# Stage B on eight narrow array tiles, with the complex products added on GpSimd

## The chip, the core and the metric

The kernel runs on one core of one Trainium2 chip. A core has a matrix engine (TensorE; PE in the profile, and PEld for its weight loads), three engines for elementwise work (VectorE: DVE, ScalarE: ACT, GpSimd: POOL), and SyncE (SP), which here only starts transfers. Transfers can be started from SP, ACT or POOL; 16 DMA engines carry all of them. Each engine takes its instructions in the order in which the program gives them, and waits where an operand is not ready. Matmul results land in PSUM, eight banks of 128 x 512 fp32. GpSimd cannot read PSUM, so what it is to work on has to be copied to SBUF first.

The metric is the device time of one execution in microseconds, as the median of some runs.

## The reference

```python
def _attn_ref(x, filt_r, filt_i):              # x: (8, 3008, 256)
    X = np.fft.rfft(x, axis=1)
    Y = X * (filt_r + 1j * filt_i)[None, :, :]  # filters: (1505, 256)
    return np.fft.irfft(Y, n=x.shape[1], axis=1)

def _moe_ref(x, w_gate, w_val, w_out):          # x: (24064, 256), d_ff = 1536
    gate = np.maximum(x @ w_gate, 0.0)
    return (gate * (x @ w_val)) @ w_out
```

Each of the eight batches is filtered along its 3008 positions through a real Fourier transform. Its 3008 x 256 result then goes, as rows, through a gated two-layer network. The output has 24064 rows of 256 fp32 values.

## The kernel before, in words

**Stages.** 3008 is split as 94 x 32. Stage A transforms along the 94, as matmuls by a cosine and sine table; its result goes through a DRAM buffer (`Abuf`) and comes back transposed as the tile `at`. Stage B, for each of 48 values of the first frequency, transforms along the 32, multiplies with the filter (a complex product) and transforms back; the result goes through a second DRAM buffer (`Dbuf`). Stage C transforms back along the 94 and writes `yT`, which is the input of the network (FFN). The FFN works in 47 blocks of 512 positions.

**Order.** The order of all work is written out by hand. After an opening (batch 0 through stages A, B and C, and the loads of weights, up to line 647), the main loop (line 689) has 47 blocks of 12 steps. One step issues `gv` (line 504: two matmuls into `psV`, two into `psG`, a copy of psV to `vsb` on ACT, and max and product into `prod` on DVE), then `o_part` (line 522: four matmuls into `psO` for the block before), and then whatever the dictionary `side` holds for that step. At steps 8 and 10 of a block, after that, `item_c` (stage C, into `psY`, line 487) makes the next block's input. `at_step(s, f)` puts work f at step s. Each batch b from 1 on has a step `end`, 72 steps after that of the batch before it, and its stages are placed by their distance to it (lines 663 to 687):

- Loads: `next_x` (line 669) at four steps, 79 to 115 steps ahead of `end`. It waits on POOL for the latest prod (`hold_gpsimd`, line 271), issues a chunk's six transfers from POOL (`load_chunk`, line 321), and then folds the chunk before it (`fold_chunk`, line 334).
- Folding: six POOL operations on a chunk of 128 x 2048 fp32, two of 128 x 1024 elements (lines 339, 340) and four of 128 x 512 (lines 341 to 344), one directly after the other.
- Stage A: `tiled_a` (line 347) four times a batch, 32 matmuls each on 32x32 tiles of the array, four copies (ACT and DVE), four stores to Abuf from SP.
- Stage B: `fwd` (line 390) at six steps, six apart (five for batch 1): eight matmuls on 64x64 tiles of the array into two banks `psX`. `product` (line 401) at that step and the next three: each is one DVE multiplication of a bank with a filter table, into `tt` (by `Ftr`) or `uu` (by `Fti`). `inv` (line 418) at the step of the next fwd: 16 matmuls, eight by `I2t` on tt and eight by `I2u` on uu, accumulated in two banks `psD`, two copies on ACT to `dsb`; every second one ends in a store to Dbuf from SP.
- `load_d` (line 466) two steps ahead of `end`: eight transfers from Dbuf on SP.

The real and imaginary rows of a filter lie twice in Ftr and Fti, as the layout of psX asks for it; in the opening `place_filter` (line 249) makes the second copy, by SP transfers, one ACT and one POOL copy. The inverse tables I2t and I2u are made in the opening from the forward table `F2` by matmuls (`make_back_t`, `make_back_u`).

**PSUM.** `bank` (line 153) gives out the eight banks in turn, the one longest free first; `done` returns a bank at its last reader in program order. psO holds one for six steps, gv takes two in each step.

**Batch 0** goes through stage B in the opening in `first_b` (line 447). It uses the same matmuls, but eight of its products are made on POOL, from copies `xs` that ACT makes of psX. Between its rounds `amid` issues some stage-A work of batch 1 (`items_a`, line 296), which reads the tiles `XF` that SP loads (`load_x`).

Of the kernel before, what the change touches and what calls it, by code (L numbers as in the profile page):

```python
# [29 lines left out]
N1, N2 = 94, 32  # L30
# [11 lines left out]
def _tables():  # L42
# [5 lines left out]
    m1 = np.zeros((NROW, N1))  # L48
# [3 lines left out]
    own = np.zeros((128, 2, 2, 64))  # L52
    order = np.arange(64).reshape(2, 32).T.reshape(64)
    for hg in range(48):
        g, a = divmod(hg, 2)
        rows = slice(a * 64, a * 64 + 64)
        e, j = g % 2, 12 * a + g // 2
        rt, ra, rm = 64 * e + j, 128 + 4 * j + 2 * e, 48 * e + j
        f = np.zeros((64, 64))
        t = np.zeros((64, 64))  # L60
        u = np.zeros((64, 64))
        k1 = 1 + g + 24 * a if hg != 47 else 0
        th = 2 * np.pi * (((n1 - 23) * k1) % N1) / N1
        wa[part, rt] = wa[part, ra] = np.cos(th)
        if k1 not in (0, 47):
# [4 lines left out]
            conj = np.tile([1.0, -1.0], 16)  # L70
            th = 2 * np.pi * (np.outer(n2, k) % S) / S
            c, s = np.cos(th), np.sin(th)
            f[:] = np.block([[c, -s], [s, c]])
            ct, st = c.T, s.T
            t[:] = np.block([[ct, st], [-st, ct]])
            u[:] = np.block([[-st, ct], [-ct, -st]]) * np.concatenate([conj, conj])[:, None]
        else:
            m1[rm] = np.cos(th) / S
            th = 2 * np.pi * (np.outer(n2, k1 + N1 * p) % S) / S
            c, s = np.cos(th), np.sin(th)  # L80
            f[0:32, 0:32:2] = c
            f[0:32, 32::2] = -s
            t[0:32:2, 0:32] = 2.0 * c.T
            t[32::2, 0:32] = -2.0 * s.T
            u[0:32:2, 0:32] = -2.0 * s.T
            u[32::2, 0:32] = -2.0 * c.T
            if k1 == 0:
                sign = np.where(n2 % 2 == 0, 1.0, -1.0)
                f[0:32, 32] = sign
                t[0, 0:32] = 1.0  # L90
                t[32, 0:32] = sign
                u[0] = 0.0
                u[32] = 0.0
        f2[lo + 64 * e, j] = f
        if g >= NG - 2:
            own[rows, 0, g - NG + 2], own[rows, 1, g - NG + 2] = t[:, order], u[:, order]
# [4 lines left out]
    swap = np.zeros((128, 128))  # L101
    conj = np.where(r % 2 == 0, 1.0, -1.0)
    swap[r ^ 32, r] = conj * np.where(r & 32, -1.0, 1.0)
    m1 = np.concatenate([m1, np.zeros((128 - NROW, N1))])
    fold = np.zeros((128, 4, 32))
    i = np.arange(24)
    for odd in range(2):
        k1 = 2 - odd + 2 * (i % 12) + 24 * (i // 12)
        if not odd:
            k1[k1 == 48] = 0  # L110
# [5 lines left out]
    tab = np.concatenate([perm, swap, own.reshape(128, -1), m1], 1)  # L116
# [4 lines left out]
def kernel(  # L121
# [52 lines left out]
    M1 = consts.tile([NROW, N1], BF16)  # L174
    F2 = consts.tile([128, NG, 64], BF16)
    I2t = consts.tile([128, NG, 64], BF16)
    I2u = consts.tile([128, NG, 64], BF16)
    Ftr = consts.tile([128, NG, D], BF16)
    Fti = consts.tile([128, NG, D], BF16)
# [15 lines left out]
    H = NG // 2  # L195
    FILT = ((filt_r, Ftr), (filt_i, Fti))
    tabs = pro.tile([128, tab_h.shape[1]], BF16, tag="tabs", bufs=1)
    perm, swap = tabs[:, 0:64], tabs[:, 64:192]

    def make_back_t(q):  # L200

        psI = [bank("psI", 4, 64) for _ in range(2)]
        for e in range(2):
            for a in range(2):
                for j in range(4):
                    nc.tensor.matmul(psI[e][64 * a:64 * a + 64, j],
                                     F2[64 * e:64 * e + 64, 12 * a + 4 * q + j, :],
                                     perm[64 * e:64 * e + 64], start=True, stop=True,
                                     tile_position=(64 * e, 64 * a))
        for e in range(2):  # L210
            nc.vector.tensor_copy(I2t[:, 8 * q + e:8 * q + 8:2, :], psI[e])
            done(psI[e])

    def make_back_u(q):

        psI = bank("psI", 8, 64)
# [39 lines left out]
    def place_nyq():  # L256
        for (src, dst), n in zip(FILT, nyq):
            nc.gpsimd.tensor_copy(dst[96:97, NG - 1, :], n)
# [471 lines left out]
```

## Time and profile before

| what | value |
|---|---|
| median of 3 runs (lowest, highest) | 891.53 us (890.38, 891.91) |
| span of the profiled execution | 885.7 us |
| around the span, to the median | 5.8 us |
| mean granted TensorE clock | 0.997 |
| first psV of the FFN at | 52.3 us |
| last output matmuls (L530) end near | 880 us |
| one batch of 72 steps in the steady part | 107 us |
| HBM | 60.42 MB read, 48.23 MB written |

The profile is of one execution on the chip, and times in it are counted from its first instruction. It gives no total for that execution beside its span, so its own time is taken as the span and the 5.8 us that lie between it and the median of the runs. In a line of it, "L433 PE MATMUL psD<-tt,I2t 64*64 64x256 bf16 x4" means: four matmuls issued by line 433, into psD, from tt and I2t, with 64 rows and 64 columns of the array, 256 columns long. What stands in brackets behind a line is how long its engine stood idle ahead of it, and whom it waited for. The start of a matmul is recorded and its end is modelled, so the cost of a group is read from its start to the start of the next one.

### The profile page before, as it was taken

Reading aid. Unit: us, or ns where it says so; the run is one execution under the profiler, and the core shown is the slowest. Engines: PE = TensorE matmul, PEld = TensorE weight load, DVE = VectorE, ACT = ScalarE, POOL = GpSimd, SP = SyncE. Lnnn points to the kernel's source line nnn. Section 1 sums busy time; section 2 is a strip of 40 time slices with the busy share of each in tenths; the row PEclk is TensorE's granted clock in tenths of the full one; section 3 lists DMA queues with packets and bytes.
Section 4 is the critical chain, followed back from the end, with each engine's and each line's share of the span. In section 5 each row is a group of like instructions: output and inputs, shape, how many; then the busy total and the mean of one; then the engine's idle time right before and its main releaser. Section 6 shows DMA issues by size and latency. Waiting matters only on the chain.

```text
span 885.7 us, 19147 instructions
## 1 busy us (share of the span) xinstructions
PE 872.1 (98%) x7190; PEld 506.9 (57%) x7190; DVE 575.7 (65%) x875; ACT 495.2 (56%) x882; POOL 376.4 (43%) x375
## 2 busy tenths in 40 slices
PE   8989999999999999999999999999999999999997
PEld 3435655666555665556655665556655666666665
DVE  4866766676666676667765776657766577655553
ACT  5734555556555655556555556555655555555552
POOL 4654796147631667216780186803866000000001
PEclk9999999999999999999999999999999999999999
DMA  9994466533645337533376234663446512421111
GB/s 242 304 221 98 155 142 146 141 117 96 150 133 124 98 101 184 129 98 98 103 179 145 81 111 133 165 125 86 123 132 142 118 46 63 105 56 31 38 34 50
DMA packets 106067, 107.28 MB, mean 121 GB/s; under 512 B 20167, under 2 KB 90087, under 8 KB 105334
## 3 DMA queue, kind: packets, MB, share of 16 engines
q1 hardware_dynamic: 81286, 76.03, 33.5%
q0 software_dynamic: 23792, 29.16, 13.3%
q8 instruction: 57, 0.93, 0.4%
q10 hardware_dynamic: 896, 0.86, 0.3%
q14 instruction: 36, 0.29, 0.1%
HBM read 60.42 MB, written 48.23 MB: 123 GB/s over the span
## 4 chain that ended last, share of the span: by engine, by line
PE 92%; DMA 4%; DVE 1%; ACT 1%; issue 0%; POOL 0%; SPq 0%; ACTq 0%; DVEq 0%
PE psV L509 27%; PE psO L530 27%; PE psG L509 26%; PE psF L353 3%; PE psY L493 2%; PE psD L433 2%; PE psX L396 2%; DMA dC<-Dbuf 2%; DMA WoT<-in_moe_w_out_dram 1%; PE psA L282 1%; DVE AT L291 1%; PE psA L303 1%; PE psJ L565 0%; DMA Dbuf<-dsb 0%; DMA Dbuf<-AS 0%
## 5 line engine op out<-in xcount | busy, mean ns | idle before, releaser
L514 DVE SCALAR_TENSOR_TENSOR prod<-psG,vsb 128x512 bf16<-128x512 f32 x564 | 388.8, 690 | 262.4 <-ACT vsb L512 257.1
L512 ACT CAST vsb<-psV 128x512 bf16<-128x512 f32 x564 | 331.9, 589 | 266.5 <-PE psV L509 179.4
L509 PE MATMUL psV<-yT,WvT 128*128 128x512 bf16 x1128 | 337.6, 380 | 0.6 <-DVE yT L500 0.6
L530 PE MATMUL psO<-WoT,prod 128*128 128x256 bf16 x2256 | 336.7, 273 | 1.1 <-DMA WoT<-in_moe_w_out_dram 1.1
L509 PE MATMUL psG<-yT,WgT 128*128 128x512 bf16 x1128 | 335.8, 379 | 0.2 <-ACT yT L498 0.2
L530 PEld LDWEIGHTS <-prod 128*128 128x128 bf16 x2256 | 220.6, 98 | 144.8 <-issue 1.5
L509 PEld LDWEIGHTS <-WgT 128*128 128x128 bf16 x1128 | 110.1, 98 | 135.6 <-issue 2.5
L509 PEld LDWEIGHTS <-WvT 128*128 128x128 bf16 x1128 | 98.6, 98 | 41.3 <-issue 30.3
L274 POOL CAST scr<-prod 128x8 f32<-128x8 bf16 x24 | 4.5, 189 | 245.0 <-DVE prod L514 245.0
L554 POOL DMA_DIRECT2D out_dram<-osb x5 | 2.6, 536 | 195.7 <-ACT osb L543 195.7
L543 ACT COPY osb<-psO 128x512 f32<-128x512 f32 x92 | 53.9, 586 | 25.9 <-PE psO L530 23.5
L412 DVE TENSOR_TENSOR tt<-psX,Ftr 128x512 bf16<-128x512 f32 x96 | 65.0, 680 | 1.6 <-POOL uu L410 0.6
L339 POOL TENSOR_TENSOR fold<-XP 128x1024 f32<-128x1024 f32 x24 | 56.5, 2354 | 19.9 <-PE psF L353 18.8
L412 DVE TENSOR_TENSOR uu<-psX,Fti 128x512 bf16<-128x512 f32 x88 | 59.8, 680 | 0.0
L326 POOL DMA_DIRECT2D XP<-in_x_dram x96 | 57.6, 603 | 3.0 <-PE psG L509 1.6
L340 POOL TENSOR_TENSOR XP<-XP 128x1024 f32<-128x1024 f32 x24 | 56.3, 2348 | 2.0
L441 ACT CAST dsb<-psD 128x512 bf16<-128x512 f32 x94 | 50.6, 591 | 11.0 <-PE psD L433 11.0
L498 ACT CAST yT<-psY 128x512 bf16<-128x512 f32 x47 | 27.5, 586 | 31.0 <-PE psY L493 30.8
L360 DVE CAST asb<-psF 128x512 bf16<-128x512 f32 x48 | 30.9, 686 | 18.6 <-PE psF L353 18.6
L360 ACT CAST asb<-psF 128x512 bf16<-128x512 f32 x48 | 25.8, 589 | 30.5 <-PE psF L353 30.5
L493 PE MATMUL psY<-M,dC 96*128 96x94 bf16 (+18 forms) x604 | 37.7, 198 | 2.8 <-DMA dC<-Dbuf 2.8
L493 PEld LDWEIGHTS <-dC 96*128 96x128 bf16 x604 | 34.4, 97 | 7.2 <-DMA dC<-Dbuf 3.2
(80 smaller groups left out, 500.9 us busy)
## 6 DMA issues: line engine op xcount, KB each, us to landing
XP<-in_x_dram POOLq DMA_DIRECT2D x48, 256.0 KB, 5.8
Dbuf<-dsb SPq DMA_DIRECT2D x23, 512.0 KB
dC<-Dbuf SPq DMA_DIRECT2D x57, 192.0 KB
XP<-in_x_dram POOLq DMA_DIRECT2D x96, 96.0 KB, 2.6
Abuf<-asb SPq DMA_DIRECT2D x96, 96.0 KB
at<-Abuf SPq DMA_DIRECT2D x24, 384.0 KB
out_dram<-osb SPq DMA_DIRECT2D x69, 94.0 KB
XF<-in_x_dram SPq DMA_DIRECT2D x15, 256.0 KB
```

The source lines that it names most:

```text
L326: nc.gpsimd.dma_start(xp[r:r + 24, 0:4:2, :], _ap(x, (b * N1 * N2 + o) * D, [[N2 * D, 24], [47 * N2 * D, 2], [1, 512]]))
L339: tt(t, xp[:, 0:2], xp[:, 2:4], op=ALU.add)
L340: tt(xp[:, 2:4], xp[:, 0:2], xp[:, 2:4], op=ALU.subtract)
L360: copy(asf[:, :, q, :], banks[q])
L412: nc.vector.tensor_tensor(p, psX, filt, op=ALU.mult)
L441: copy(dsb[:, a, o:o + 2, :], psD[a])
L493: nc.tensor.matmul(psY[:, o:o + w], dCs[b, n2 // 8][:, n2 % 8, h * 128:(h + 1) * 128], M1[:, n1:n1 + w], start=True, stop=True)
L509: nc.tensor.matmul(pt[:, :W], w[:, h, ft * 128:(ft + 1) * 128], yt[:, h, :], start=(h == 0), stop=(h == 1))
L512: nc.scalar.copy(vsb, psV[:, :W])
L514: nc.vector.scalar_tensor_tensor(prod, in0=psG[:, :W], scalar=0.0, in1=vsb, op0=ALU.max, op1=ALU.mult)
L530: nc.tensor.matmul(psO[:, t % 2], prods[ft][:, t * 128:(t + 1) * 128], WoT[:, ft, :], start=(ft == 0), stop=(ft == NFT - 1))
L543: copy(osb[:, t0 % 2:t % 2 + 1], psO[:, t0 % 2:t % 2 + 1])
```

## The change

- **Forward (batches 1 to 7).** Three forwards a batch instead of six. Each is 32 matmuls on eight 64x32 tiles, real and imaginary part in separate banks: four banks, for two halves e of the rows and two parts. ACT copies the two banks of e=1 to SBUF (`xs`, fp32) and gives them back at once.
- **Products and adds.** Eight DVE products a forward, one in each of eight successive steps, now with fp32 result (`qr`). After each second one POOL adds or subtracts the pair into `y` (bf16). So y is the finished complex product.
- **Inverse.** Three a batch, ten steps after their forward: 32 matmuls on eight 32x64 tiles, one pass over y with one table IT, into four banks; two ACT and two DVE copies, one store.
- **Batch 0** keeps products without adds, on the new tiles: four terms a pair with tables IT and its negative ITN.
- **Filters** are stored once, with 20 POOL transfers in two halves; no copies, no extra rows. The tables are made by `make_back`, on PE, DVE and ACT. Two small SP transfers (`hold_sync`) hold the loads of batch 1's x behind the filters.
- **Folding.** A chunk is loaded by four transfers of 128 rows, at steps of its own; its six POOL operations are spread over eight steps (at 0, 2, 4, 5, 6, 7), in a new order, in place. The clearing of XP (four memsets) goes.

```diff
-    def place_filter(fi, a, half, copy):
...
+    def make_back():
+        psI = {}
+        for t in range(2):
+            for e in range(2):
+                psI[t, e] = bank("psI", 3, 2, 64)
...
+            for e in range(2):
+                gs = slice(6 * t + e, 6 * t + 6, 2)
+                nc.vector.tensor_copy(IT[:, gs], psI[t, e])
+                nc.scalar.mul(ITN[:, gs], psI[t, e][:, :, 0], -1.0)
...
+    def hold_sync(tile_):
+        scr = sb.tile([128, 32], BF16, tag="scs", bufs=2)
+        nc.sync.dma_start(scr[:tile_.shape[0]], tile_)
...
     def load_chunk(b, j):
-        xp = XP[j]
-        for q in range(4):
...
+        xp, o = XP[j], (b * N1 * N2 + 2 * j) * D
+        for i in range(4):
+            up = N2 * D if i % 2 == 0 else -N2 * D
+            nc.gpsimd.dma_start(xp[:, i, :],
+                                _ap(x, o + (46 * (i % 2) + 47 * (i // 2)) * N2 * D,
+                                    [[8 * D, 4], [up, 32], [1, 512]]))
+    def fold_steps(b, j):
+        xp, st = XP[j], {}
+        tt = nc.gpsimd.tensor_tensor
+        def differences():
+            st["d"] = fs.tile([128, 2, 512], FP32, tag="fold", bufs=1, name="fold")
+            tt(st["d"], xp[:, 0:2], xp[:, 2:4], op=ALU.subtract)
+        yield differences
+        yield lambda: tt(xp[:, 0:2], xp[:, 0:2], xp[:, 2:4], op=ALU.add)
+        yield lambda: tt(xp[:, 2], xp[:, 0], xp[:, 1], op=ALU.add)
+        yield lambda: tt(xp[:, 3], xp[:, 0], xp[:, 1], op=ALU.subtract)
+        yield lambda: tt(xp[:, 0], st["d"][:, 0], st["d"][:, 1], op=ALU.add)
+        yield lambda: tt(xp[:, 1], st["d"][:, 0], st["d"][:, 1], op=ALU.subtract)
...
+    def fwd(b, r):
+        ps_ = psXs[b, r] = {(e, comp): bank("psX", 2, D) for e in range(2) for comp in range(2)}
+        for m in range(2):
+            for comp in range(2):
+                for cg in range(4):
+                    for e in range(2):
+                        forward(b, ps_[e, comp][32 * cg:32 * cg + 32, m], 6 * cg + 2 * r + m, comp, e, cg)
+        for comp in range(2):
+            xs = fs.tile([128, 2, D], FP32, tag="xs", bufs=2, name="xs")
+            nc.scalar.copy(xs, ps_[1, comp])
+            done(ps_[1, comp])
+            ps_[1, comp] = xs
+    def product(b, r, e, n):
+        comp, k = ((0, 0), (1, 1), (0, 1), (1, 0))[n]
+        p = fs.tile([128, 2, D], FP32, tag="qr", bufs=6, name="qr")
+        nc.vector.tensor_tensor(p, psXs[b, r][e, comp], FILT[k][1][:, 4 * r + e:4 * r + e + 3:2, :], op=ALU.mult)
+        qr[n % 2] = p
+        if n % 2:
+            y = fs.tile([128, 2, D], BF16, tag="y", bufs=6, name="y")
+            nc.gpsimd.tensor_tensor(y, qr[0], qr[1], op=ALU.add if n // 2 else ALU.subtract)
...
+    def inv(b, r):
+        psD = [bank("psD", 2, D) for cg in range(4)]
+        dsb = sb.tile([128, 4, 2, D], BF16, tag="dsb", bufs=3, name="dsb")
+        for m in range(2):
+            inverse(b, psD, r, m, ((0, 0), (1, 1)))
+        evacuate(dsb, psD, slice(0, 2))
...
+        store_d(b, r, dsb, 0, 2)
...
+    hold_sync(Fi[:, 5, D - 32:])
+    load_x(1, nc.sync, ((0, 0, 4 * q),))
+    hold_sync(Fi[:, 11, D - 32:])
     load_x(1, nc.sync, ((1, 0, 4 * q),))
...
         if b > 1:
-            for j, e in enumerate((-74, -69, -62, -55) if b == 2 else (-74, -69, -64, -57)):
-                l = (22, 29, 34, 43)[j] if b == 2 else end - 115 + NFT * j
...
+                at_step((12, 20, 29, 40)[j] if b == 2 else end + (-134, -120, -104, -90)[j], next_x)
+                l = (20, 31, 42, 53)[j] if b == 2 else end + (-124, -109, -94, -81)[j]
+                for n, f in zip((0, 2, 4, 5, 6, 7), fold_steps(b, j)):
+                    at_step(l + n, f)
+                e = (-74, -68, -62, -55)[j] if b == 2 else (-74, -69, -64, -57)[j]
                 at_step(end + e, lambda b=b, j=j: tiled_a(b, j))
             at_step(end + e + 4, lambda b=b: load_at_tiled(b))
...
+        for r in range(3):
+            lf, li = ((-36, -26), (-25, -15), (-14, -4))[r] if b == 1 else ((-38, -28), (-26, -16), (-14, -4))[r]
+            at_step(end + lf, lambda b=b, r=r: fwd(b, r))
+            for n in range(8):
+                at_step(end + lf + n, lambda b=b, r=r, n=n: product(b, r, n // 4, n % 4))
+            at_step(end + li, lambda b=b, r=r: inv(b, r))
```

`forward` issues one matmul on a 64x32 tile; `inverse` issues, for each table and part, eight matmuls on the eight 32x64 tiles (four groups of rows, two of columns), the parts in the order real, imaginary; `evacuate` copies four banks, ACT and DVE in turn. Where two pieces of work have the same step, that of the lower batch comes first.

## The prediction

> **What bounds the kernel now.** I read the page's busy shares first, then the chain that ended last, then the busy time by stretch, and last the instructions in order of time on PE and on POOL.
>
> From the page: busy time by engine, and the chain by engine.
>
> ```profile
> PE 872.1 (98%) x7190; PEld 506.9 (57%) x7190; DVE 575.7 (65%) x875; ACT 495.2 (56%) x882; POOL 376.4 (43%) x375
> ...
> PE 92%; DMA 4%; DVE 1%; ACT 1%; issue 0%; POOL 0%; SPq 0%; ACTq 0%; DVEq 0%
> ```
>
> One batch takes 107 us in the steady part. Busy time by stretch there (stretch, length, then PE, PEld, DVE, ACT, POOL, the granted clock, DMA):
>
> ```profile
> 334.00:441.00 107.00, 107.00 (x929) 62.74 (x928) 71.94 (x111) 61.64 (x111) 53.62 (x51) 1.00 0.48 122
> ```
>
> PE has no idle time in it. So an edit gains only PE time, and it loses as soon as PE has to wait for anything. PE in order of time (start, then duration of the merged group):
>
> ```profile
> 405.24 0.60 PE L530 MATMUL psO<-WoT,prod 128*128 128x256 bf16 x4
> 405.77 0.41 PE L396 MATMUL psX<-at,F 64*64 64x256 bf16 x8
> 406.01 0.28 PE L433 MATMUL psD<-tt,I2t 64*64 64x256 bf16 x4
> ...
> 406.34 0.28 PE L433 MATMUL psD<-uu,I2u 64*64 64x256 bf16 x4
> 406.55 0.60 PE L509 MATMUL psV<-yT,WvT 128*128 128x512 bf16 x2
> ...
> 407.43 0.60 PE L530 MATMUL psO<-WoT,prod 128*128 128x256 bf16 x4
> 407.86 0.59 PE L509 MATMUL psV<-yT,WvT 128*128 128x512 bf16 x2
> ...
> 441.50 0.30 PE L433 MATMUL psD<-tt,I2t 64*64 64x256 bf16 x4
> ...
> 442.06 0.61 PE L509 MATMUL psV<-yT,WvT 128*128 128x512 bf16 x2
> ```
>
> Start to start: an output group followed by psV takes 0.43-0.44 us, followed by a tiled group 0.53, so entering costs 0.09. An FFN step is 1.30 (406.55 to 407.86). Eight psX matmuls take 0.24 ahead of psD; alone, the trace has 0.35. Sixteen psD matmuls take 0.54 behind psX and 0.56 (441.50 to 442.06) alone. Four matmuls on four 64x64 tiles cost 0.11 together.
>
> POOL in order of time, one chunk's loads and its folding:
>
> ```profile
> 437.92 0.19 POOL L274 CAST scr<-prod 128x8 f32<-128x8 bf16 x1 [3.62 <-DVE prod L514]
> 439.72 2.41 POOL L326 DMA_DIRECT2D XP<-in_x_dram  x4 [1.62 <-PE psG L509]
> 442.13 1.40 POOL L330 DMA_DIRECT2D XP<-in_x_dram  x2
> 446.08 2.35 POOL L339 TENSOR_TENSOR fold<-XP 128x1024 f32<-128x1024 f32 x1 [2.55 <-PE psF L353]
> 448.51 2.35 POOL L340 TENSOR_TENSOR XP<-XP 128x1024 f32<-128x1024 f32 x1
> 450.94 1.27 POOL L341 TENSOR_TENSOR XP<-fold 128x512 f32<-128x512 f32 x1
> 452.28 1.29 POOL L342 TENSOR_TENSOR fold<-fold 128x512 f32<-128x512 f32 x1
> ```
>
> A wide fold operation occupies POOL 2.43 us start to start, a narrow one 1.34, a 256 KB load 0.70 of issue. Today only tiled_a, many steps later, waits for POOL.
>
> **PE work of stage B.** Per batch now: 7 entries into tiled mode (0.65), psX 5 x 0.242 + 0.345 = 1.56, psD 5 x 0.539 + 0.563 = 3.26; together 5.47 us. After: three forward groups of 32 matmuls on eight 64x32 tiles and three inverse groups of 32 on eight 32x64 tiles, never adjacent. If eight run in the 0.11 that four take, each is four such rounds, the lone psD group's 0.563, plus 0.093 to enter: 6 x 0.656 = 3.94. Gain 1.53, over seven batches **-10.7 us**. The bound on the other side is four at a time: each group then has four more rounds, 1.09, the six 6.56, a loss of 1.1 a batch, +7.6. I take the gain, since psF, on sixteen 32x32 tiles, needs 1.07 us for 32 fp32 matmuls of 512 columns (chain) where psA needs 3.43 for 8: those tiles do run together.
>
> The Trainium skill, "TensorE: Matmul & The Clock Gate" (its section "Wait — 56ns, not 53.3ns?"), speaks against this: start to start never drops below about 25 ns, so 32 small matmuls would need 0.80 us. The trace disagrees, with psD starts 3 ns apart within a round. By the rule six groups would cost an estimated 6 x (0.09 + 0.80 + 0.10) = 5.9 and the gain would turn into a loss of about 3 us in all.
>
> **The new link: PE waits for POOL.** The inverse now reads y, which POOL adds from two DVE products. Four adds per group, each priced by the 1.34 of L341 (L410, one bf16 input, is 1.16; the choice moves 0.2 an add). They enter the queue that already carries folds and loads, and the inverse that waits holds up every matmul behind it, hence ACT's vsb, DVE's prod and all output.
>
> Work one steady group, r=0 of batch b-1, while batch b (3 to 7) is folded. A chunk's loads are now four issues instead of six (2.8 us for 3.8), moved to other steps than its folding. Count steps from its forward (end-110 in b's counting), time 0 at that step's first matmul. Step 1 starts at 1.96; two stage-C items add 0.25 each; the inverse at step 10 wants all four adds at about 15.7. DVE's second, fourth, sixth and eighth product are ready at 5.1, 7.1, 9.7, 12.3 (prod about 1.25 us into a step, ACT first copying two xs at 0.48 a piece, DVE at 0.61 an operation; the DVE lines come at that spacing in first_b). POOL's order by the due steps, with the end of each: y0 6.4 | differences 8.8, y1 10.2 | sums 12.6, y2 13.9 | narrow 15.3 | narrow 16.6, hold and four loads 19.7 (0.25 + 4 x 0.70) | y3 21.05. **PE stands 5.3 us.** Without those loads it would be 2.3; without the folds it would be zero (y3 at 15.4). For r=1 the same tally ends at 0.2, for r=2 at none: fewer folds lie before y3. Five batches (b-1 = 2 to 6): 5 x 5.5 = 27.5. Batch 1, with its own due steps and one load set in each group: 2.2, 2.4, 2.4, together 7.0. Batch 7 has no folding beside it: 0. Sum **+34.5**.
>
> **What such a wait does to the clock.** Near 50 us PE waits 2.35 us for dC; the stretches around it:
>
> ```profile
> 48.20:50.40 2.20, 0.00 (x0) 0.00 (x0) 0.67 (x1) 0.00 (x0) 0.00 (x0) 1.00 1.02 312
> 51.41:54.82 3.41, 3.41 (x8) 1.06 (x7) 1.47 (x3) 0.68 (x2) 3.41 (x6) 0.50 0.88 125
> ```
>
> The clock is then 0.50 for 3.41 us, a loss of up to 1.7. Each of the eight long waits costs between 0 and 1.7 (13.6 in all); how much of the half-clock stretch falls into the wait itself is open, so I take the middle, **+6.8**.
>
> **DVE, ACT and PSUM.** DVE keeps 24 products a batch, now eight steps in a row: 2 x 0.61 per 1.30 step fits. Six of twelve dsb copies move there (6 x 0.61). ACT loses six and gains six xs copies. A forward takes four banks at once, but two return after the xs copies. SP still stores three slabs of Dbuf a batch. Cost zero, covered by DVE's 65%; if the cover fails, a lag of about 0.3 us for 21 forwards, +6.
>
> **End of batch 1.** Its last inverse comes one step later (end-4 for end-5), and psY already waits 0.45 us for dC there: **+1.3** (0 if earlier loads free the DMAs). Other batches keep end-4.
>
> **The opening, before the first psV at 52.** Filters take 20 POOL issues instead of 12 (8 x 0.55 = 4.4 us); the last ends near 23, before psX at 28. Six SP copies, two 2.7 us filter copies, the memsets and make_back_u (0.65) go; that gains nothing while the transposes (4.2 each) follow the last psA, paced by XF. The 7.1 us XP memset lies beside FFN steps. Two small SP transfers now hold the second batch's XF loads behind half the filters, and XF[0] goes as one piece; the first item reads it at 29.2, so 0 to 2 late. Forward and inverse change tile shape in each round, about 0.1-0.2 x 5. Bounds -1 and +4; I take **+1**.
>
> **Sum.** -10.7 + 34.5 + 6.8 + 1.3 + 1.0 = +32.9. The profiled span is 885.7; launch and end add 5.8 to the median 891.5 of the three runs. 891.5 + 32.9 = 924.
>
> **Rivals.**
> - *POOL keeps up* (other sign). y3 lands before the inverse because POOL's issue and adds overlap more than their rows. For it: POOL is busy only 43%. Against it: the rows follow each other without overlap, and 16 us of POOL work stands where 10.6 fit. It decides once that work shrinks by a third. Then -10.7 + 2.3 = 883; partial waits reach up to 905.
> - *DVE blocks POOL's port.* Half of the products now read two SBUF operands, which no row here does beside POOL. If POOL stood still for their four 0.61 us, 2.4 us more in some thirteen groups that are already late or nearly so: +31, 955; half of it is 940. The Trainium skill's "GPSIMD Engine Reference" (section 1, Specifications) names such contention with two SBUF inputs. In the trace a fold stays at 2.35 beside PSUM-reading DVE work, which tests it not.
> - *Tiles run four at a time.* +7.6 for -10.7 turns 924 into 942; the psF row speaks against it.
>
> **Chances.** Forecast 0.50 (own range 908 to 936), POOL keeps up fully or in part 0.33, port 0.11, four at a time 0.06. The keeping-up case splits into 0.29 under 889.7, little within 0.2% of the median (about what a measurement of this kernel can tell from no change), the rest above. The range 882 to 940 leaves out about a tenth at each end. Faster 0.28, same 0.03, slower 0.69.
>
> **What would show it.** Right: PE waiting on POOL's y in the list of waits, some 5 us at one inverse per batch and nothing in the last batch; POOL's load issues between the third and fourth add; the clock at 0.50 after them; groups of 32 at 0.56. Wrong: no such wait, POOL's y starting straight after its product, or tiled groups of 0.8 us and more. The weakest step is the price of POOL's queue.

## The result, and the profile after

The changed kernel takes 959.85 us (median of 4 runs, 957.96 to 964.30) where the kernel before takes 891.53: 1.077 times as long, interval 1.073 to 1.081. The forecast was 924, with 940 as the upper end of its range. The direction was right, the size was not: 68 us came where 33 were expected. The profiled execution has a span of 956.2 us against 885.7, so 70.5 us are to be found in the trace. A run that lies over 1.5% above the fastest of its kernel counts as slow and is left out of a median; this concerns four runs of one experiment below.

The page of the changed kernel: busy time by engine, the granted clock in 40 slices, and the chain by engine.

```profile
PE 883.8 (92%) x7593; PEld 507.7 (53%) x7715; DVE 665.9 (70%) x917; ACT 488.9 (51%) x879; POOL 463.0 (48%) x412
...
PEclk9899999998999989999999989999899999999999
...
PE 57%; POOL 14%; issue 12%; DVE 8%; DMA 6%; ACT 2%; SPq 0%; ACTq 0%; POOLq 0%; DVEq 0%
```

PE carried 92% of the chain before and carries 57% now; POOL, DVE and "issue" have come in. DVE is busy for 90 us more (575.7 before). Its 50 copies of psD (the evacuation that moved there) take 31 us of that; the rest must be operations that have become longer. The clock is below its highest digit in five slices.

The waits of PE in the changed kernel (who waited for whom: us in total, times, longest):

```profile
PE psD L351 <- POOL y L451: 25.9, 7, 4.8
PE psD L351 <- DVE prod L519: 10.8, 20, 1.2
PE psV L514 <- DVE yT L505: 6.6, 3, 4.0
PE psX L340 <- DMA at<-Abuf: 4.4, 1, 4.4
```

The first line is the one that the prediction asked for. The next two name DVE, which the prediction had put at nothing, and the fourth is a transfer that it did not mention.

**One steady inverse, r = 0 of batch 5.** POOL in order of time:

```profile
554.13 1.27 POOL L451 TENSOR_TENSOR y<-qr 128x512 bf16<-128x512 f32 x1 [9.63 <-DVE qr L447]
555.36 2.36 POOL L292 TENSOR_TENSOR fold<-XP 128x1024 f32<-128x1024 f32 x1
557.66 1.73 POOL L451 TENSOR_TENSOR y<-qr 128x512 bf16<-128x512 f32 x1
559.35 2.80 POOL L294 TENSOR_TENSOR XP<-XP 128x1024 f32<-128x1024 f32 x1
562.11 1.71 POOL L451 TENSOR_TENSOR y<-qr 128x512 bf16<-128x512 f32 x1
563.79 1.71 POOL L295 TENSOR_TENSOR XP<-XP 128x512 f32<-128x512 f32 x1
565.46 1.26 POOL L296 TENSOR_TENSOR XP<-XP 128x512 f32<-128x512 f32 x1
566.67 0.18 POOL L231 CAST scr<-prod 128x8 f32<-128x8 bf16 x1
566.80 2.70 POOL L281 DMA_DIRECT2D XP<-in_x_dram  x4
569.52 1.27 POOL L451 TENSOR_TENSOR y<-qr 128x512 bf16<-128x512 f32 x1
```

This is the order of the prediction's tally to the letter: the fourth sum stands behind two narrow folds, the hold and four loads. But four of the ten have grown, a sum from 1.27 to 1.73 or 1.71, a wide fold from 2.36 to 2.80, a narrow one to 1.71.

PE in order of time, at that inverse and at the next one (r = 1):

```profile
565.62 0.37 PE L351 MATMUL psD<-y,IT 32*64 32x256 bf16 x9 [0.30 <-DVE prod L519]
570.84 0.85 PE L351 MATMUL psD<-y,IT 32*64 32x256 bf16 x20 [4.84 <-POOL y L451]
...
575.54 0.63 PE L340 MATMUL psX<-at,F 64*32 64x256 bf16 x32
576.10 0.61 PE L514 MATMUL psV<-yT,WvT 128*128 128x512 bf16 x2
...
590.09 0.29 PE L351 MATMUL psD<-y,IT 32*64 32x256 bf16 x1
591.45 0.29 PE L351 MATMUL psD<-y,IT 32*64 32x256 bf16 x2 [1.07 <-DVE prod L519]
592.04 0.73 PE L351 MATMUL psD<-y,IT 32*64 32x256 bf16 x29 [0.30 <-DVE prod L519]
```

A gap is read here from start to start of neighbouring matmuls inside the group. At r = 0 it is 5.11 us in each of batches 2 to 6. The psX group of 32 takes 0.56 from its start to psV, as forecast. At r = 1 PE does not wait for a sum at all: of the four banks that psD was given, one was psG two steps ago and one was psG a step ago, and `prod`, the DVE operation that reads them, is late. So two gaps follow each other, 1.36 and 0.59 us, in each of the five batches. At r = 2 the longest gap is 0.59 in four batches and 1.42 in one.

Why DVE is late stands in its own order of time, at the products of that r = 1 and with POOL's beside them:

```profile
581.35 0.68 DVE L519 SCALAR_TENSOR_TENSOR prod<-psG,vsb 128x512 bf16<-128x512 f32 x1
581.95 1.38 DVE L447 TENSOR_TENSOR qr<-xs,Fr 128x512 f32<-128x512 f32 x1
583.25 0.68 DVE L519 SCALAR_TENSOR_TENSOR prod<-psG,vsb 128x512 bf16<-128x512 f32 x1
583.85 2.23 DVE L447 TENSOR_TENSOR qr<-xs,Fi 128x512 f32<-128x512 f32 x1
...
588.57 2.23 DVE L447 TENSOR_TENSOR qr<-xs,Fr 128x512 f32<-128x512 f32 x1
590.72 1.27 DVE L519 SCALAR_TENSOR_TENSOR prod<-psG,vsb 128x512 bf16<-128x512 f32 x2
```

```profile
582.74 2.80 POOL L292 TENSOR_TENSOR fold<-XP 128x1024 f32<-128x1024 f32 x1
586.23 1.26 POOL L451 TENSOR_TENSOR y<-qr 128x512 bf16<-128x512 f32 x1 [0.69 <-DVE qr L447]
587.45 2.79 POOL L294 TENSOR_TENSOR XP<-XP 128x1024 f32<-128x1024 f32 x1
```

A product of two SBUF operands begins at 583.85 and ends at 586.08, half a microsecond after the fold that began at 582.74 has ended (585.54). The fold began while the product before it (581.95 to 583.33) still ran, and took 2.80. So each seems to hold until the other is through. The whole trace bears this out: 68 of the 84 products from xs begin while a fold or sum runs on POOL, and 65 of them end 0.55 us after that operation's end; of the other 16, 14 take 0.67 to 0.68. Folds and sums that begin while such a product runs mostly take 0.3 to 0.5 us more (37 of 40), the others keep to 1.25 to 1.28 or 2.34 to 2.36. Over the whole trace, by groups (line, engine, operation, operands, count, then busy time and mean ns):

```profile
L447 DVE TENSOR_TENSOR qr<-xs,Fr 128x512 f32<-128x512 f32 x42 | 66.6, 1585 | 0.0
...
L447 DVE TENSOR_TENSOR qr<-xs,Fi 128x512 f32<-128x512 f32 x42 | 59.1, 1406 | 0.0
...
L447 DVE TENSOR_TENSOR qr<-psX,Fr 128x512 f32<-128x512 f32 x42 | 28.8, 685 | 8.1 <-PE psX L340 7.0
```

The same multiplication takes 0.685 us from PSUM and 1.4 to 1.6 from SBUF in the mean. The 84 products from SBUF hold some 68 us more of DVE than at 0.68 a piece. In batch 7, where there is nothing to fold, products from xs are 0.68 long when POOL stands still and 1.45 when a sum runs.

**The clock behind the long gap.** Busy time by stretch (stretch, length, PE, PEld, DVE, ACT, POOL, the granted clock, DMA share, GB/s):

```profile
564.74:570.84 6.10, 0.96 (x13) 0.34 (x13) 2.03 (x4) 0.58 (x1) 6.08 (x9) 0.71 0.33 72
570.84:574.14 3.30, 3.08 (x27) 1.56 (x28) 1.81 (x3) 1.61 (x3) 2.38 (x2) 0.50 1.01 183
574.14:577.84 3.70, 3.65 (x51) 2.03 (x50) 1.64 (x4) 2.15 (x4) 0.00 (x0) 1.00 1.00 191
```

Between 1.3 and 4.1 us after PE falls idle in each gap of 5.11 us, the clock goes to 0.50 for 6.83 us. Here about half of that lies in the gap and 3.3 us behind it; in the other batches 3.7 to 6.0 us lie behind it. The sum over the trace of (1 - clock) times PE's busy time, taken in short pieces, comes to 14.2 us after the first psV; before, the same sum gives 1.3.

**The account.** First psV: 61.5 for 52.3, +9.2. First psV to the last output group: 890.3 for 827.4, +62.9. Behind it: -1.6. The list of waits understates the inverses: it counts a wait from the modelled end of the matmul before it, about 0.3 us after that matmul's start. Read from start to start instead, from each inverse's first matmul to the next piece of work, the 21 inverse groups hold 50.0 us above 0.57 a piece, where the list has 36.7. With that, the 62.9 are the gain in PE work (-10.7), the inverses (+50.0), the waits for yT and for `at` (+11.0) and the clock while PE works (+12.9 by the sum above). These make 63.2; the half clock inside an inverse is counted twice in it.

### The profile page after: what moved, and what is told of

Same layout as the page of the kernel before. It is cut to its first block, busy times and chain, and to the rows that moved or that the text cites. A ratio compares the mean times of both kernels' runs of the same rounds, so it can differ in the third digit from the quotient of the medians.

```text
span 956.2 us, 20067 instructions
## 1 busy us (share of the span) xinstructions
PE 883.8 (92%) x7593; PEld 507.7 (53%) x7715; DVE 665.9 (70%) x917; ACT 488.9 (51%) x879; POOL 463.0 (48%) x412
## 4 chain that ended last, share of the span: by engine, by line
PE 57%; POOL 14%; issue 12%; DVE 8%; DMA 6%; ACT 2%; SPq 0%; ACTq 0%; POOLq 0%; DVEq 0%
PE psO L535 17%; PE psG L514 17%; PE psV L514 16%; DVE prod L519 5%; POOL XP L281 3%; POOL y L451 3%; DVE qr L447 3%; PE psF L306 3%; PE psD L351 2%; ACT vsb L517 2%; POOL fold L292 2%; DMA XF<-in_x_dram 2%; POOL XP L294 1%; POOL XP L296 1%; DMA XP<-in_x_dram 1%
## 5 line engine op out<-in xcount | busy, mean ns | idle before, releaser
L514 PE MATMUL psG<-yT,WgT 128*128 128x512 bf16 x1088 | 331.2, 383 | 5.7 <-ACT dsb L360 1.1
L514 PE MATMUL psV<-yT,WvT 128*128 128x512 bf16 x1048 | 322.7, 383 | 7.9 <-DVE yT L505 6.6
L451 POOL TENSOR_TENSOR y<-qr 128x512 bf16<-128x512 f32 x84 | 111.8, 1332 | 203.4 <-DVE qr L447 193.5
L281 POOL DMA_DIRECT2D XP<-in_x_dram x96 | 65.0, 682 | 4.0 <-DMA at<-Abuf 2.0
L447 DVE TENSOR_TENSOR qr<-xs,Fr 128x512 f32<-128x512 f32 x42 | 66.6, 1585 | 0.0
L351 PE MATMUL psD<-y,IT 32*64 32x256 bf16 x672 | 26.7, 306 | 36.7 <-POOL y L451 25.9
L447 DVE TENSOR_TENSOR qr<-xs,Fi 128x512 f32<-128x512 f32 x42 | 59.1, 1406 | 0.0
L360 ACT CAST dsb<-psD 128x512 bf16<-128x512 f32 (+1 forms) x50 | 26.0, 572 | 52.7 <-PE psD L351 52.7
L360 DVE CAST dsb<-psD 128x512 bf16<-128x512 f32 (+1 forms) x50 | 31.0, 659 | 29.9 <-PE psD L351 29.8
L351 PEld LDWEIGHTS <-IT 32*64 32x64 bf16 x816 | 14.9, 111 | 52.7 <-issue 46.5
```

What stands on the lines that cost most here:

```text
L281: nc.gpsimd.dma_start(xp[:, i, :], _ap(x, o + (46 * (i % 2) + 47 * (i // 2)) * N2 * D, [[8 * D, 4], [up, 32], [1, 512]]))
L351: nc.tensor.matmul(psD[cg][64 * e:64 * e + 64, m], ITN[rows, slot, :] if tab == 2 else IT[rows, slot, tab, :], terms[b, r, m, e, comp][row ...
L360: copy(dsb[:, cg, ms], psD[cg][:, ms])
L447: nc.vector.tensor_tensor(p, psXs[b, r][e, comp], FILT[k][1][:, 4 * r + e:4 * r + e + 3:2, :], op=ALU.mult)
L451: nc.gpsimd.tensor_tensor(y, qr[0], qr[1], op=ALU.add if n // 2 else ALU.subtract)
L514: nc.tensor.matmul(pt[:, :W], w[:, h, ft * 128:(ft + 1) * 128], yt[:, h, :], start=(h == 0), stop=(h == 1))
```

## The experiments

The runs of one comparison share a chip with runs of the kernel before, whose median there was 889 to 891 us. Where nothing else is said, an edit is made on the changed kernel.

### Chunk loads 8 steps earlier

```diff
-   ... end + (-134, -120, -104, -90)[j], next_x)
+   ... end + (-134, -120, -112, -90)[j], next_x)
```

> The changed kernel with one of four chunk loads a batch (the third, batches 3 to 7) issued eight steps earlier, before the forward instead of between the third and the fourth add of its first group. Queue theory (POOL's order alone sets when y3 is there): the gap of 5.1 us at the first inverse of five batches shrinks by the 2.85 us that hold and loads take, to about 2.3; 5 x 2.8 = 14 us less, and up to 5 x 1.5 more if the clock then stays at 1.0: span 935 to 942 for 956. Rival (the waits come from slow DVE products and DMA issue costs POOL nothing that matters): the gap stays at 5.1, span 956.

949.9 us (two runs, 944.1 and 955.6). With the loads ahead of the sums instead of between the third and the fourth, the gap at r = 0 is 2.25 us in batches 3 to 6 instead of 5.11, and those at r = 1 and r = 2 are mostly as they were (1.36, 0.59); at r = 2 two batches have 1.42 or 1.43. The tally of the queue is right in this. The list of waits has 11.0 us for POOL's sums in place of 25.9:

```profile
PE psD L351 <- POOL y L451: 11.0, 7, 2.0
```

The time fell by 10 us where 14 to 21 were expected, and the two runs lie 11 us apart. The first forward of batch 2 now waits 9.5 us for `at`, probably because the earlier transfers run beside it.

### All folds outside the sums

```diff
-   ... (-134, -120, -104, -90)[j], next_x)         l = ... (-124, -109, -94, -81)[j]
+   ... (-145, -140, -134, -127)[j], next_x)        l = ... (-133, -125, -117, -75)[j]
```

(Two lines of the code, the loads and the folds, are printed side by side here and below.)

> The changed kernel with all loads and folding of batches 3 to 7 moved to steps at which no stage B of the batch before runs. Queue theory: no gap at the inverses of batches 2 to 6, as at those of batch 7 now: their groups return from 6.9, 2.6 and 1.6 us to 0.57, five times 9.4 = 47 us less, and some 5 us more as the clock stays up: span 903 to 910. Port theory (a DVE product with two SBUF operands and a POOL operation take turns) expects the same here, but also that the products from xs still take 1.45 us wherever a y add runs, and 0.68 elsewhere. Rival (PE's gaps come from the width of the tiles or from PSUM): gaps stay.

962.4 us: nothing gained where some 50 us were expected, though nearly every gap ahead of an inverse went. The waits of PE:

```profile
PE psX L340 <- DMA at<-Abuf: 27.8, 7, 7.9
PE psY L498 <- DMA dC<-Dbuf: 19.9, 6, 5.2
```

Four chunks of 1 MB now run in 18 steps beside the stores of stage A, the load of `at` and the loads from Dbuf; the DMA engines stand at a share of 1.06 (400 to 420 us). The wait has changed its owner. It also shows that without a fold beside them the products from SBUF make no gap at r = 1 and r = 2, though they still take 0.67 to 3.46 us, 1.0 to 1.3 in the median.

### All products from PSUM

```diff
-        for comp in range(2):
-            xs = fs.tile([128, 2, D], FP32, tag="xs", bufs=2, name="xs")
-            nc.scalar.copy(xs, ps_[1, comp])
-            done(ps_[1, comp])
-            ps_[1, comp] = xs
...
-        if n == 3 and e == 0:
+        if n == 3:
             for comp in range(2):
-                done(psXs[b, r][0, comp])
+                done(psXs[b, r][e, comp])
```

> The changed kernel without the xs copies: all eight products read PSUM, the four banks are given back when read. So no DVE product has two SBUF operands. Port theory: all products take 0.68 us; the gaps at the second and third inverse of a batch (1.36 and 0.59) go, the one at the first shrinks by the 0.45 us or so that each of three POOL operations lost, to about 4; no psV waits for DVE's yT (6.6 us now): 5 x 3.1 + 5 x 1 + 6 = 25 us less, span about 930. Queue theory without the port: gaps at the second and third inverse stay, span 950 to 956. Against both: four banks held for eight steps leave gv three; if that binds, psV waits for DVE's prod in each of 21 forwards, up to 10 us back.

923.8 us (921.8 to 925.8), 36 less. The gaps at r = 1 and r = 2 are gone (the group takes 0.57, once 1.28), the wait for yT falls from 6.6 to 0.3, and only one psX waits for a bank, 0.8 us. The gap at r = 0 is 3.8 to 3.9 us in place of 5.1 (3.0 in batch 2), those of batch 1 are 1.3 to 1.7. So this is what POOL's queue costs by itself:

```profile
PE psD L351 <- POOL y L446: 20.9, 9, 3.7
```

Between first psV and last output group 35.6 us have gone: the inverse groups have 25.4 of them (24.6 above 0.57 a piece, for 50.0), the wait for yT 6.3 and the half clock 4.0.

### The same, with ScalarE's copies left in place

The edit above took two things away, DVE's reads of SBUF and 42 copies on ScalarE. Here, of the five lines that went, only the last two (`done` and the assignment) go, so that the copies are made and read by nobody.

> The changed kernel with the ScalarE copies xs left in place, but nobody reads them: all products read PSUM, and the banks come free after the eighth product, as in the run with 923.8 us. It asks whether that run gained by VectorE's reads or by ScalarE's copies that were gone. Theory (a product with both operands in SBUF and a GpSimd addition hold each other up): as without the copies, 918 to 928 us, no gaps at r = 1 and r = 2. Rival (the eight copies of 2.4 us in a batch held up ScalarE and with it the evacuations): 945 to 960 us, gaps as in the changed kernel.

926.5 us (924.8 to 928.2), within the scatter of the run without copies. The groups of this run:

```profile
L445 DVE TENSOR_TENSOR qr<-psX,Fr 128x512 f32<-128x512 f32 x84 | 57.4, 684 | 7.9 <-PE psX L340 6.8
L445 DVE TENSOR_TENSOR qr<-psX,Fi 128x512 f32<-128x512 f32 x84 | 57.2, 681 | 0.0
L437 ACT COPY xs<-psX 128x512 f32<-128x512 f32 x42 | 22.6, 589 | 23.2 <-PE psX L340 23.2
```

ScalarE spends its 22.6 us on the copies and it costs next to nothing; DVE's 168 products take 0.68 each. The gaps at r = 1 are gone; of those at r = 2 one, in batch 2, is 2.1 us, and its cause is open. Nor is it the banks: by the order in which the program gives them out, psD gets banks from batch 2 on that were psV and psG one and two steps ago, in this kernel as in the changed one. What cost 33 to 36 us is where DVE reads from.

### The opening: no holds on SP

Both `hold_sync` lines are taken out, so that no part of x for batch 1 waits for a filter.

> The changed kernel without the two small SP transfers that hold the loads of batch 1's x until the filters are there. If the hold makes the opening late: the wait of PE for XF at its first item (3.0 us) goes, and with it the half clock that follows (34.8 to 41.6 us): first psV at about 56 instead of 61.5, span 951. If the filters themselves set the pace and the loads only compete with them: the products or the first psA wait for the filters instead, first psV at 60 to 63, span 955 to 958.

954.2 us, but the first psV comes at 62.7, not earlier. PE no longer waits 3.0 us for x; it waits 4.3 us for a product made on POOL, whose filter is late instead. The 5 us less lie behind the first psV: the half clock takes 10.4 us there, for 14.2.

A first psV has to be read with its scatter. Seven of the profiled kernels here have the changed kernel's opening line for line, and theirs lie between 59.5 and 63.7 us.

### The opening: ten filter transfers

```diff
-        direct(*FILT[0], 0, 6)
-        yield
-        conj(*FILT[0], 0, 6)
-        direct(*FILT[1], 0, 6)
-        conj(*FILT[1], 0, 6)
-        for src, dst in FILT:
-            direct(src, dst, 6, 12)
-            conj(src, dst, 6, 12)
+        for src, dst in FILT:
+            direct(src, dst, 0, 12)
+            conj(src, dst, 0, 12)
+        yield
...
-    next(filters)
-    hold_sync(Fi[:, 5, D - 32:])
+    hold_sync(Fr[:, 11, D - 32:])
```

> The changed kernel with the filters loaded in 10 transfers (all twelve groups at once, 384 KB and 96 KB) instead of 20, none of them ahead of the first rows of x; the second wait of SP is moved onto the first filter, so that nothing of x waits for half a filter. Theory (the small, early transfers make the opening late): the first product of stage A starts at 7.6 to 8 us again instead of 10.3, the half clock at 10.9 goes, the second filter is complete by 28 us, and the first psV comes at 55 to 58 us instead of 61.5; the time falls by 3 to 6 us. Rival (the bytes of the filters and of x set it, or the 1 KB pieces of the mirrored half do): the first product is early, but the first psV stays at 60 to 62 us and the time within 2 us.

959.6 us (956.0 to 963.1), first psV 61.5: the same. PE in order of time:

```profile
8.05 3.60 PE L235 MATMUL psA<-XF,WA 128*128 128x512 f32 x8
...
28.96 0.41 PE L336 MATMUL psX<-AT,F 64*32 64x256 bf16 x16 [0.48 <-DVE AT L244]
...
35.48 1.99 PE L256 MATMUL psA<-XF,WA 128*96 128x512 f32 x2 [5.22 <-DMA XF<-in_x_dram]
```

Stage A starts at 8.05 instead of 10.29 and stage B at 29.0 instead of 31.6, as the theory had it; nearly all of it is given back in a wait for x of 5.2 us, which was 3.0. Half of the theory holds, and the gain is off the path that sets the first psV.

### PE kept busy in the long gap

```diff
+        if r == 0 and b > 1:
+            for i in range(21):
+                nc.tensor.matmul(psD[3]..., WoT[:, 0, 0:128], WgT[:, 0, 0:512], start=True, stop=True)
         for m in range(2):
             inverse(b, psD, r, m, ((0, 0), (1, 1)))
```

> The changed kernel with 21 matmuls of 512 columns on constants (4.5 us, results overwritten) on PE ahead of the inverse of r = 0 in batches 2 to 7, where PE stood for 5.1 us in batches 2 to 6. No wait is taken away: PE only isn't idle in it. Batch 7, which has no such wait, loses the 4.5 us. Theory (the half clock that follows each of the five waits costs up to 3.4 us each, 17 us in all): the clock stays at 1.00 behind those five, and the time falls by 5 to 13 us to 947 to 955. Rival (the clock's loss is 0 to 1.7 us a wait as the prediction had it, and mostly lies in the wait): 0 to 8 less for five waits against 4.5 more for batch 7, 956 to 965.

958.3 us (956.1 to 960.7). Busy time by stretch, at one filled gap and behind it:

```profile
216.75:222.44 5.69, 5.43 (x52) 2.35 (x52) 1.15 (x2) 0.33 (x1) 5.67 (x8) 1.00 0.44 91
222.44:226.00 3.56, 3.51 (x53) 2.01 (x51) 2.87 (x5) 2.38 (x5) 1.94 (x2) 1.00 1.04 161
```

The clock stays at 1.00 through and behind the gaps, so the half clock comes from PE's idleness there. But the time fell by 1.5 us only, which is within the scatter of the runs, and the total is the rival's. The theory had counted all of the 6.83 us, of which a part lies in the wait; and the half clock has appeared at other places, behind three gaps of 1.36 to 2.1 us at r = 1, which had a full clock behind them in the changed kernel, and near 60 and 98 us. By the same sum over pieces, PE loses 14.2 us over the whole span here and 18.8 in the changed kernel (opening included): 4.6 gained, and 4.5 paid in batch 7.

Why the short gaps now bring the half clock, and did not before, stays open in part. The traces show one thing that bears on it. In each of them the half-clock stretches begin whole multiples of 3.413 us apart: 219.13, 335.18, 451.24 and 567.29 in the changed kernel, 34 such pieces from one to the next. Cut all fourteen traces into these pieces (but for the first 5 and the last 7 us). The clock fell 76 times, each time behind a piece in which PE had been busy for at most 0.60 of the time. It fell behind all 59 pieces at full clock with PE busy for less than 0.42; behind those between 0.42 and 0.61 it fell 17 times and stayed 47 times. So how a gap lies on this grid matters, and gaps of 1 to 2 us are at the edge.

### Products from PSUM, loads and folds ahead of r = 0

On the kernel with all products from PSUM:

```diff
-   ... (-134, -120, -104, -90)[j], next_x)         l = ... (-124, -109, -94, -81)[j]
+   ... (-140, -132, -112, -90)[j], next_x)         l = ... (-130, -121, -94, -81)[j]
```

> All products from PSUM (as in the run with 923.8 us), and the loads and folds of the first two chunks ahead of the first forward group: loads at -140, -132, -112, -90 instead of -134, -120, -104, -90 steps, folds at -130, -121, -94, -81 instead of -124, -109, -94, -81; so no fold and no load stands in POOL's queue among the sums of r = 0. Theory (the rest of the loss is POOL's queue, 5 gaps of 3.8 us with the half clock behind them): the gaps of r = 0 fall below 1 us, the half clock at them goes, and the time falls by 18 to 27 us to 896 to 906. Rival (as when all folds stood outside: the transfers collide): the gaps go, but PE waits for at and dC by 10 us or more, and the time stays at 912 to 924.

899.6 us (median of four runs, 890.4 to 900.3; four more reach 906.6), as the theory had it. The gaps at r = 0 are gone: every group at r = 0 of batches 2 to 7 takes 0.57 or 0.58, and all but two at r = 1 and r = 2. In the profiled run the first forward of batch 2 waits 8.6 us for `at`, in two pieces of 2.2 and 6.4, with a stretch of 10.2 us at half clock of which 5 lie behind the wait. That place seems to be what scatters: the fastest run has a mean clock of 0.998, the other seven 0.988 to 0.992. But only one run was profiled.

### The same with ten filter transfers

> Both edits of the two runs before this one together. Theory (opening and POOL queue are separate): the gains add, 891 to 902 us, first psV at 55 to 58 us. Rival: no more than the spread alone gives, within 2 us of it.

888.5 us (8 runs, 884.7 to 889.5), the same as before the change: 0.999, interval 0.997 to 1.000. The first psV is 1.0 us earlier (60.0 for 61.0), which is within its scatter, and batch 2 no longer waits for `at`. Most of the 11 us is therefore not the opening's own time; why `at` is now in time was not tried by itself.

### The opening in another order

On top of that:

```diff
-        for src, dst in FILT:
-            direct(src, dst, 0, 12)
-            conj(src, dst, 0, 12)
+        src, dst = FILT[0]
+        conj(src, dst, 0, 12, (0, 1))
         yield
+        direct(src, dst, 0, 12)
+        conj(src, dst, 0, 12, (2, 3))
+        direct(*FILT[1], 0, 12)
+        conj(*FILT[1], 0, 12)
...
+    next(filters)
...
-    hold_sync(Fr[:, 11, D - 32:])
     load_x(1, nc.sync, ((0, 0, 4 * q),))
-    hold_sync(Fi[:, 11, D - 32:])
+    hold_sync(Fr[:, 11, D - 32:])
     load_x(1, nc.sync, ((1, 0, 4 * q),))
```

> On top of the version with 888.5 us (all products from PSUM, loads and folds spread, ten filter transfers): two of the mirrored transfers go out ahead of the first rows of x, so that POOL's queue need not stop for 7 us in the middle of the filters; the first piece of x for the second batch waits for no filter, the second for the first filter. Theory (the opening's loss is the wait of SP and the stop of POOL's queue): the wait of 5.2 us for x falls to 0 to 2 us, first psV at 54 to 57 us instead of 60.0, the time 882 to 886 us. Rival (the bytes set it): PE then waits for a product with the second filter instead, first psV at 59 to 62 us, 887 to 891 us.

885.5 us (885.1 to 888.0), 0.995 of before (0.993 to 0.997); first psV 58.1, at the edge between the two (60.2 and 58.5 in the next two kernels, which have the same opening). POOL's queue no longer stops, and the wait for x is gone; 3.0 us of waits for products, held up behind the second filter, have come in its place (psD at 33.2, 33.8 and 35.0).

### Batch 1's sums between the folds

```diff
-   (12, 20, 29, 40)[j] if b == 2 ...               l = (20, 31, 42, 53)[j] if b == 2 ...
+   (10, 14, 25, 36)[j] if b == 2 ...               l = (22, 33, 44, 53)[j] if b == 2 ...
```

> The same, and the second batch's own chunks laid between the sums of batch 1: loads at steps 10, 14, 25, 36 instead of 12, 20, 29, 40, folds from 22, 33, 44, 53 instead of 20, 31, 42, 53. Theory (POOL's queue makes batch 1's three gaps of 1.3 to 1.7 us): they fall below 0.6 us, 3 to 4 us less than the run before it. Rival: in batch 1 POOL has too much work in any order, and the gaps stay within 0.5 us of what they are, the time within 1 us.

883.4 us (8 runs, 880.9 to 887.4), 0.994 of before (0.991 to 0.996): the fastest version here, 0.6% under the kernel before. It is 2.0 us under the run before it, where 3 to 4 were expected, and the two overlap in their runs. Two of batch 1's three gaps (2.8, 1.4 and 1.3 in the run before it) are gone, the third is 0.9 us. This is one batch's 107 us of it, by stretch, the same stretch that the prediction showed of before:

```profile
334.00:441.00 107.00, 106.10 (x972) 62.54 (x988) 78.09 (x119) 59.29 (x106) 66.06 (x58) 1.00 0.57 130
```

PE is all but full again at a full clock, with 66 us of POOL beside it.

### The copies put back into the fastest version

> The best version so far (883.4 us) with the copies xs and the products from SBUF put back as in the changed kernel. It asks whether the products from SBUF still cost time when no fold and hardly a load stands between the sums. Theory (they hold up POOL's additions, and are held up by them): products of 1.3 to 1.6 us beside an addition, gaps of 0.5 to 1.5 us ahead of the inverses in batch 1 and at r = 1 and r = 2, half the clock behind some of them, 892 to 910 us. Rival (POOL then has slack enough): within 3 us of 883.

909.7 us (907.5 to 911.1), 26 more for five lines. No gap at r = 0, where no fold stands beside the products; at r = 1, where folds do, 1.36 again, and at r = 2 0.59 in three batches, 0.86 and 1.58 in two. The waits of PE:

```profile
PE psD L350 <- DVE prod L518: 9.1, 17, 1.1
PE psD L350 <- POOL y L450: 3.1, 3, 1.3
PE psV L513 <- DVE yT L504: 2.8, 3, 1.3
```

By the sum over pieces the half clock takes 3.2 us here and 3.1 without the copies, so the 26 us are not the clock's. A steady batch is 3.8 us longer than without the copies, and some 3.3 of that is in its inverse groups: 2.62 us at r = 1 and 1.54 to 2.18 at r = 2, for 0.57. Over the trace the 21 groups hold 19.5 us above 0.57 a piece, for 1.2 without the copies. The expectation said 892 to 910 with half clock behind some of the gaps; the size came without it.

## Why the prediction was right or wrong

A steady batch, from the first psF to the first psF of the next one, is the clearest measure. Most of them take 106.8 us before, 116.5 to 117.6 after, 105.3 in the fastest version and 108.7 to 109.4 in that with the copies put back.

- **PE work of stage B (-10.7): right.** Groups of 32 take 0.56 to 0.58 us where nothing is waited for. The fastest version's batch is 1.5 us shorter than before, where 1.53 was forecast for a batch. Eight tiles do run together, and the rival with four at a time falls. The 25 ns from start to start of the Trainium skill ("TensorE: Matmul & The Clock Gate", section "Wait — 56ns, not 53.3ns?") do not hold between matmuls on different tiles: 32 in 0.56 us is 17.5 ns each, with the entry included.
- **POOL's queue (+34.5): the mechanism right, the size by luck.** The order in the queue was met to the operation, and 5.1 us stood where 5.3 were forecast. But the queue alone, without products from SBUF, gives 3.8 to 4.3 us at r = 0 (2.9 to 3.0 in batch 2), none at r = 1 and one or none at r = 2, and 1.3 to 1.7 in batch 1 where 2.2 to 2.4 were forecast: 25 us above 0.57 a group in all, 28 with the copies left in place. In the tally the narrow operations and sums were put at 1.34 us; without the collision they follow one another at 1.22 to 1.23. The rest of the 5.1 is the collision.
- **"DVE, ACT and PSUM ... Cost zero": this is the step that failed.** It named DVE's 65% as cover and priced a product at 0.61 for any operand. Products from SBUF take 1.4 to 1.6 us in the mean, and DVE's lateness comes back to PE by a way that the text had not followed: `prod` frees the banks in which psD begins. By the experiments this costs 33 to 36 us in the changed kernel and 26 in the fastest version. The rival "DVE blocks POOL's port" was this mechanism, priced at 31 us and thus 955, and given a chance of 0.11; the range ended at 940, the half of it. Its reason, "no row here" does it, was an open cost and not an argument for a small one; the text called the port's contention untested and then let the range leave it out. What the Trainium skill says of two SBUF inputs ("GPSIMD Engine Reference", section 1, Specifications), that the two engines then contend, is borne out by 1.4 to 1.6 us against 0.685. In detail the rival was off too: it had POOL stand still for 0.61 us a product, while it is mostly DVE that stands, until POOL's operation has ended. A sum or fold grows by 0.45 in the rows shown and a product by 0.7 to 1.5.
- **The clock (+6.8): mis-sized.** The bound of 1.7 us a wait came from one wait of 2.35 us, followed by 3.41 us at 0.50. In the changed kernel a wait of 5.1 us brings 6.83 us at 0.50, of which 3.3 to 6.0 lie behind the wait, a loss of 1.6 to 3.0; and shorter waits bring it too. After the first psV it comes to +12.9 us, about twice the term.
- **The opening (+1, at most +4): wrong, 9.2** in the profiled execution, 7.2 to 11.3 over the seven with this opening. The sum had taken POOL's issue time, to end at 23 us before psX, and not the time at which the transfers land. POOL's last filter issue ended at 27.5, after a stop of 3.5 us between two of them. Between 16 and 28 us the core's transfers move 110 GB/s where 248 were moved before, and x, held behind the filters, comes late. Fewer and earlier transfers and looser holds brought the first psV to 58.1 to 60.2 in three kernels, some 2.4 us earlier in the mean; what keeps the other 6 us or so is partly 3.0 us of waits behind the second filter, and beyond that open.
- **End of batch 1 (+1.3): did not come.** No wait for dC is listed there. Instead batch 2's first forward waited 4.4 us for `at`. A chunk's loads, moved to an earlier step, run beside it, and the text had costed that move on POOL's queue only, not on the DMA engines. That they are the cause is likely and was not tried by itself.
- **The rival "POOL keeps up" (883):** it is the fastest version, in which hardly anything of POOL's is late (0.6 us in the list of waits). The bound of the change, taken without its side effects, was right for the work behind the opening: from first psV to last output group it takes 817.4 us for 827.4, -10.0. That the total of 883.4 us meets the 883 so closely is luck: in its profiled execution the first psV is 7.9 us late, where the sum had 1, and 1.9 us are won behind the last output group, which the sum did not have.

Of the signs that the text asked for, all that were to show it right are there, in the right places. They showed that its mechanism ran; they could not show that it was the only one.

## What to carry to other kernels

Before moving an operand of VectorE from PSUM to SBUF to free a bank, look for what GpSimd does at that time: the copy itself cost nothing here, the place that VectorE then read from cost 26 to 36 us. When a step is slow, follow it through the buffers that it frees as well as through its result, and cost a moved load on the DMA engines too, not only in the queue that issues it. A resource that no row shows in use is a term with a wide bound in the range, and when a first experiment removes a wait without gaining time, the list of waits says who owns it now.

## What was not expected of the hardware

- A DVE multiplication with both operands in SBUF and a GpSimd operation beside it lengthen each other: DVE 0.68 to 1.4 and 2.2 us, POOL 1.27 to 1.7 and 2.35 to 2.8. A product that begins while POOL's operation runs ends 0.55 us behind it, in 65 of 68 cases. With one operand in PSUM both keep their times (0.68 to 0.69 in 46 products beside POOL; 1.27 and 2.35).
- The half clock began whole multiples of 3.413 us apart and lasted 3.41 us, or two or three times that. Behind a gap of 5.1 us it lasted 6.83 each time in the changed kernel, but 3.41 behind two of the four such gaps of the kernel without holds. Behind gaps of 1.4 us it came in some runs and not in others.
- In the opening POOL stood for 3.5 us between two filter transfers, and for 6.8 to 7.2 with ten of them, until one of the earlier ones had landed; with two of them issued ahead it did not stand. So the number of open transfers seems to be bounded; which bound it is was not tried.
